# A list-scheduled attention and MLP kernel: the planner learns that VectorE and GpSimd exclude each other

## The chip, the cores and the metric

The kernel runs on one core of a Trainium2 chip. TensorE (PE in the profile) multiplies matrices and writes PSUM, VectorE (DVE) and ScalarE (ACT) read and write PSUM and SBUF, GpSimd (POOL) works on SBUF alone, and SyncE (SP) issues most of the DMAs. Each engine takes its instructions strictly in the order in which they stand in its queue. The metric is the device time of one execution in microseconds.

## The reference

Everything is fp32: 8 batches, 8 heads, 576 positions, head size 64, model size 512, hidden size 2048.

```python
kv  = einsum('bhsd,bhse->bhde', k, v)            # per head 64 x 64
o   = einsum('bhsd,bhde->bhse', q, kv)
x   = o / sqrt(mean(o*o, -1) + 1e-6) * g_norm    # heads side by side: 576 x 512
a1  = alpha1 * x + beta1
u   = x + lam * einsum('ts,bsd->btd', w_tok, a1) # token mixing, 576 x 576
a2  = alpha2 * u + beta2
out = u + lam * (relu(a2 @ w_ch1) @ w_ch2)
```

## The kernel before

**Stages of a batch.** k and v are loaded and rounded (`round_kv`, to `kr` and `vr`), and TensorE forms kv (`kv_groups`, L563). For batches 0 and 1 q is transposed on TensorE in fp32. From batch 2 on q is split into two bf16 halves: `split_q` writes the high half on ScalarE and the remainder, a subtraction, on VectorE or GpSimd (L510); `qt_dma` transposes both halves by DMA (L517). `qkv_groups` multiplies q by kv for two chunks of 128 positions at a time (a last one has 64), and then runs a chain: the square on ScalarE (L682), its sum on VectorE (L684), square root (L687), reciprocal (L690), the normalised x on VectorE (L706), `rt` = x times alpha1 lam g_norm as bf16 (L710), and at last x times g_norm in place on GpSimd (L712). `tok_groups` mixes the tokens: it needs all five chunks of `rt` and the transposed w_tok `wt` (L740); the result is added to x on VectorE (L722) and multiplied by alpha2 to `a2b` (L726), which `ut_groups` transposes to `a2t`. `ch1_groups` makes the hidden layer (L855 for even batches, L870 for odd ones, which also carry the tails of two batches; L886 for a first part of batch 0), with bias and relu on ScalarE or VectorE (L844, L845). `ch2_groups` multiplies by lam w_ch2 (L919), adds u (L928) and stores.

**How batches interleave.** While the hidden layer of batch b runs, the attention chain of batch b+1 is mixed in; then come the token mixing of b+1 and the second layer of b, into which the roundings, the q split and kv of batch b+2 are merged. So at each change of batch the chain up to `rt` of the next batch has to be finished when TensorE has come through the hidden layer.

**Head.** Batch 0 is handled in two halves of four heads. w_tok is loaded in natural order and cast to bf16 (`wt_groups`, part `cast`); the cast permutes columns so that every fourth column stands together, two more casts take the last 64 columns, and TensorE transposes 128 x 128 pieces (L1076, L1093). w_ch1 comes in four loads into three staging slots and is cast by whichever of three engines suits (L1173 and the cast behind it); w_ch2 likewise, multiplied by lam (L1186, L1191). Until the first hidden-layer matmul can start, the planner fills TensorE with dummy matmuls (L1265).

**What sets the order.** Nothing of this order is written out by hand. `Prog.op` records each operation with its engine or engines, an estimated cost for each, and its dependencies. `Prog.schedule` plays the operations through in model time: an engine that is free takes the ready operation of the lowest priority number (in SyncE's opening loads, strictly the first; TensorE looks at most eight ahead). Where several engines can do it, `better_elsewhere` asks whether another would be through sooner; GpSimd or VectorE operations carry a handicap of 0.7 us for VectorE (`spare`). `hasten` puts everything that the first hidden-layer matmuls depend on in the order of its remaining path, and `soon` keeps an engine free for such an operation. The plan's order becomes the queue of each engine; semaphores are added afterwards, so the order is fixed before the program runs and doesn't react to what happens on the chip. PSUM banks are handed out by the plan too.

Costs in microseconds for n elements per partition (the planner's own):

```python
def dve_us(n, mode=1): return 0.16 + n / 960.0 / mode
def act_us(n):         return 0.19 + n / 1200.0
def pool_us(n):        return 0.15 + n * 0.0024
def dve_pool(n):       return {"DVE": dve_us(n) + 0.08, "POOL": pool_us(n)}
```

In the plan VectorE and GpSimd work side by side without any effect on each other.

Of the kernel before, what the change touches and what calls it, by code (L numbers as in the profile page):

```python
# [9 lines left out]
ALU = mybir.AluOpType  # L10
# [12 lines left out]
class Op:  # L23
    __slots__ = ("eng", "cost", "fn", "deps", "alloc", "tiles", "pri", "idx",
                 "start", "end", "pos", "fixed", "waits", "inc", "lat", "ring", "clock")

    def __init__(self, eng, cost, fn, pri, idx):
        self.eng, self.cost, self.fn, self.pri, self.idx = eng, cost, fn, pri, idx
        self.deps, self.fixed = set(), False
# [20 lines left out]
class Prog:  # L50
# [20 lines left out]
    def op(self, eng, cost, fn, r=(), w=(), pri=0.0, dma_us=None, at=None, after=()):  # L71
# [3 lines left out]
        o.lat = dma_us  # L75
# [47 lines left out]
    def schedule(self):  # L123
# [10 lines left out]
        dma_free = 0.0  # L134
# [223 lines left out]
def bass_transnormer_attn__then__resmlp_affine_kernel(  # L358
# [15 lines left out]
    with ExitStack() as stack:  # L374
# [63 lines left out]
        def pool_us(n):  # L438
            return 0.15 + n * 0.0024
# [27 lines left out]
        def load_tail(n, b, at=None):  # L467
# [4 lines left out]
                w=[key], dma_us=1.2, at=at)  # L472
# [10 lines left out]
        def round_kv(b, parts=ALL, after=()):  # L483
            for i, hs in enumerate(parts):
                m = 256 * (hs.stop - hs.start)
                aa = halves(hs)
                for src, dst, lo, n in ((kf, kr, 0, "k"), (vf, vr, 64, "v")):
                    o, s = dst[:, 0:4, hs, :], src[:, hs].rearrange("p h c d -> p c h d")
                    ot, st = dst[0:64, 4, hs, :], kft[lo:lo + 64, hs]
                    P.op(act_dve(m, 1.7) if b < R32 else "DVE", dve_us(m, 1.7),  # L490
                         lambda e, o=o, s=s: copy(e, o, s),
                         r=[(n + "f", a) for a in aa], w=[(n + "r", a, 0) for a in aa],
                         after=after)
                    P.op(act_dve(m // 4, 1.7) if b < R32 else "DVE", dve_us(m // 4, 1.7),
                         lambda e, o=ot, s=st: copy(e, o, s),
                         r=[n + "ft"], w=[(n + "r", a, 1) for a in aa],
                         after=after)

        def split_q(b):

            lo_, par = 64 * (b % 2), b % 2
            for c in range(5):
# [8 lines left out]
                    out=lo, in0=src, in1=hi, op=ALU.subtract), r=kin + [kh], w=[kl])  # L511
# [43 lines left out]
        def kv_groups(b):  # L555
            def group(a):
# [35 lines left out]
                for h in range(2):  # L592
# [7 lines left out]
                        r=[("kvd", a, h, 0), ("kvd", a, h, 1)], w=[("kvd", a, h, 2)])  # L600
# [21 lines left out]
        def qkv_groups(b):  # L622

            def group(cs, hs):
# [74 lines left out]
                else:  # L699
# [9 lines left out]
                P.op(dve_pool(64 * m) if b else "DVE", dve_us(64 * m),  # L709
                     lambda e: e.tensor_tensor(out=r_, in0=x, in1=eb, op=ALU.mult),  # L710
                     r=xk + ["e1"], w=[("rt", rc(b, c), a) for a in aa for c in cs], pri=-100)
# [6 lines left out]
        def tok_out(b, c, t):  # L718
# [5 lines left out]
            if b == 0 and c < 4:  # L724
# [3 lines left out]
                r=xk + ["a2"], w=[("a2b", c) if c < 4 else ("a2bt", b % 2)])  # L728
# [237 lines left out]
        def params():  # L966
            P.op("DVE", 0.69, lambda e: e.tensor_tensor(
                out=e1r, in0=e1r, in1=lamr, op=ALU.mult), r=["lamr", "e1r"], w=["e1r"])
# [83 lines left out]
        def wt_groups():  # L1052
            def cast(tc):
                rr = 128 if tc < 4 else 64
                o = wsb[0:rr, tc, 0:512].rearrange("p (c s) -> p c s", c=4)
                i = wst[0:rr, tc, 0:512].rearrange("p (s c) -> p c s", c=4)
                P.op({"POOL": 0.75, "DVE": 0.75, "ACT": 0.65}, 0, lambda e: copy(e, o, i),
                     r=[("wst", tc)], w=[("wsb", tc)])

            def cast_tail(rr, tcs):  # L1060
                P.op({"POOL": 0.4, "DVE": 0.4, "ACT": 0.4}, 0, lambda e: copy(
                    e, wsb[0:rr, tcs, 512:576], wst[0:rr, tcs, 512:576]),
                    r=[("wst", tc) for tc in range(tcs.start, tcs.stop)],
                    w=[("wsbt", tcs.start)])
            for tc in range(5):
                yield lambda tc=tc: cast(tc)
            yield lambda: cast_tail(128, slice(0, 4))
            yield lambda: cast_tail(64, slice(4, 5))

            def group(tc):  # L1070
# [3 lines left out]
                def f(e):  # L1074
                    for sc in range(4):
                        m = e.transpose(  # L1076
                            t.flat().bitcast(BF16)[:, 128 * sc:128 * sc + rr],
                            wsb[0:rr, tc, 128 * sc:128 * sc + 128], identb[0:rr, 0:rr])
                    return m
# [7 lines left out]
            def group_tail():  # L1087
# [9 lines left out]
                P.op("PE", 0.35, f, r=["identb", ("wsbt", 0), ("wsbt", 4)], w=[t])  # L1097
# [65 lines left out]
        for key in ([("wst", x) for x in range(5)] + ["smask", ("wsbt", 0), ("wsbt", 4)] +  # L1163
# [7 lines left out]
        def load_w(i):  # L1171
            if i < 4:
# [4 lines left out]
                for dj in range(4):  # L1177
# [3 lines left out]
                        r=[("stg", i % 3)], w=[("w1p", i, dj)], at=-960.0 + i)  # L1181
                P.lastw[("w1", i)] = [y for dj in range(4) for y in P.lastw[("w1p", i, dj)]]
                bias_groups(i)
            else:
# [5 lines left out]
                for hh in range(4):  # L1190
# [3 lines left out]
                        after=u0)  # L1194
# [104 lines left out]
```

## Time and profile before

| what | us |
|---|---|
| median of three runs (397.54 to 399.26) | 398.19 |
| the profiled execution | 397.5 |
| span in that execution, first to last instruction | 395.4 |
| TensorE busy | 369.6 |
| VectorE busy | 252.5 |
| GpSimd busy | 148.5 |
| ScalarE busy | 147.6 |

A row such as "L510 DVE TENSOR_TENSOR qs<-qf,qs" names the line of the kernel, the engine, the operation and what it writes from what. In a timeline the first number is the start and the second the duration, both in microseconds; brackets show how long the engine had been idle just before and what ended that idle time. In the chain that ended last, pieces are given as start, duration and what ran. The time of an instruction on VectorE or GpSimd includes the time in which it has started but stands still. Casts and copies made through the helper `copy` carry L449 on ScalarE and L450 on the others, whatever they belong to; the tile names tell them apart (`kr`, `vr`, `wt`, `w`; w_tok's staging and bf16 copy lie in the memory of `ht` and are named so; the tails of k and v share the tile `kft`).

### The profile page before, as it was taken

To read this page: it belongs to the slowest core of one execution; us is meant where nothing else is said; L and a number is where in the kernel's file an instruction comes from. 1 tells how busy PE (TensorE), PEld (TensorE's weight loads), DVE (VectorE), ACT (ScalarE), POOL (GpSimd) and SP (SyncE) were. 2 spreads that over 40 slices of the span, in tenths; PEclk is the share of its full clock that TensorE was granted. 3 is DMA by queue.
4 is the path that set the end of the run, shared out by engine and by line. 5 is a ranking of instruction groups with operands and counts; after the bars stand their busy time and mean duration, and the time that the engine had idled before them with its cause. 6 is when DMAs were issued, how large, how long until landed. Compare 5 with 4: busy or idle time off the path is not lost.

```text
span 395.4 us, 5965 instructions
## 1 busy us (share of the span) xinstructions
PE 369.6 (93%) x2543; PEld 216.5 (55%) x2303; DVE 252.5 (64%) x367; ACT 147.6 (37%) x262; POOL 148.5 (38%) x108
## 2 busy tenths in 40 slices
PE   6999989879799899799988999899999999999995
PEld 4578766336564365346753465346774465447642
DVE  6569889998684648873799248873765248620021
ACT  1665646212753027501770017501760047006600
POOL 7357257970585303550175002650084005610000
PEclk9879999989999999999998999999999999999999
DMA  8987999768998539892975219832442110140012
GB/s 193 301 320 171 362 373 257 214 156 161 281 214 196 164 109 228 154 188 79 236 164 138 76 54 234 165 82 67 102 61 60 73 55 2 26 120 28 0 55 80
DMA packets 93948, 59.27 MB, mean 150 GB/s; under 512 B 60306, under 2 KB 84894, under 8 KB 93922
## 3 DMA queue, kind: packets, MB, share of 16 engines
q1 hardware_dynamic: 93888, 58.88, 60.3%
q8 instruction: 19, 0.31, 0.3%
q14 instruction: 7, 0.06, 0.0%
q10 hardware_dynamic: 34, 0.02, 0.0%
HBM read 38.04 MB, written 9.44 MB: 120 GB/s over the span
## 4 chain that ended last, share of the span: by engine, by line
PE 63%; DVE 14%; DMA 13%; ACT 3%; issue 2%; POOL 2%; SPq 1%; POOLq 0%
PE ps L919 26%; PE ps L870 11%; PE ps L740 9%; PE ps L855 7%; DMA stg<-in_moe_w_ch_dram 6%; DMA qf<-in_q_dram 6%; PE ps L563 4%; DVE qs L510 3%; DVE rt L710 2%; DVE small L684 2%; DMA qt<-qs 2%; DVE xm L706 2%; DVE w L1191 1%; PE ps L960 1%; PE ps L641 1%
## 5 line engine op out<-in xcount | busy, mean ns | idle before, releaser
L919 PE MATMUL ps<-w,ht 128*128 128x512 bf16 x576 | 131.4, 382 | 1.8 <-DVE xm L928 1.6
L919 PEld LDWEIGHTS ps<-w,ht 128*128 128x128 bf16 x576 | 55.3, 98 | 67.6 <-DVE xm L928 2.1
L844 ACT ACTIVATE ht<-ps,bias 128x640 bf16<-128x640 f32 (+2 forms) x98 | 71.0, 737 | 46.1 <-PE ps L870 36.5
L870 PE MATMUL ps<-a2t,w 128*128 128x320 bf16 x512 | 72.2, 299 | 2.6 <-ACT ht L844 1.6
L928 DVE TENSOR_TENSOR xm<-ps,xm 128x512 f32<-128x512 f32 x32 | 22.1, 690 | 70.4 <-PE ps L919 70.2
L870 PEld LDWEIGHTS ps<-a2t,w 128*128 128x128 bf16 x512 | 49.2, 98 | 23.0 <-ACT ht L844 2.6
L710 POOL TENSOR_TENSOR rt<-xm,e_bc 128x1024 bf16<-128x1024 f32 x7 | 16.5, 2355 | 116.6 <-DVE xm L706 116.6
L855 PE MATMUL ps<-a2t,w 128*128 128x512 bf16 x240 | 54.8, 379 | 1.7 <-ACT ht L844 1.7
L740 PE MATMUL ps<-rt,wt 128*128 128x512 bf16 x180 | 42.1, 391 | 8.9 <-DVE rt L710 5.3
L590 ACT ACTIVATE kvd<-ps 64x128 bf16<-64x128 f32 x24 | 6.5, 271 | 106.2 <-PE ps L563 106.1
L712 POOL TENSOR_TENSOR xm<-xm,g_bc 128x1024 f32<-128x1024 f32 (+1 forms) x18 | 40.8, 2266 | 12.6 <-DVE rt L710 11.8
L855 PEld LDWEIGHTS ps<-a2t,w 128*128 128x128 bf16 x240 | 22.5, 98 | 27.5 <-ACT ht L844 2.6
L740 PEld LDWEIGHTS ps<-rt,wt 128*128 128x128 bf16 x180 | 17.5, 100 | 32.1 <-DVE rt L710 6.6
L845 DVE TENSOR_SCALAR ht<-ps,bias 128x512 bf16<-128x512 f32 (+2 forms) x34 | 24.9, 747 | 8.9 <-PE ps L855 4.4
L684 DVE TENSOR_REDUCE small<-sq 128x16 f32<-128x1024 f32 (+3 forms) x27 | 25.0, 933 | 5.4 <-ACT sq L682 5.3
L563 PE MATMUL ps<-vr,kr 128*128 128x256 f32 x160 | 24.4, 301 | 3.4 <-DVE vr L450 3.4
L722 DVE TENSOR_TENSOR xm<-ps,xm 128x512 f32<-128x512 f32 x28 | 19.0, 686 | 11.7 <-PE ps L740 11.4
L726 POOL TENSOR_TENSOR a2b<-xm,a_bc 128x512 bf16<-128x512 f32 x15 | 19.4, 1291 | 17.1 <-DVE xm L722 16.9
L563 PEld LDWEIGHTS ps<-vr,kr 128*128 128x128 f32 x160 | 21.4, 193 | 6.0 <-DVE vr L450 4.2
L682 ACT ACTIVATE sq<-ps 128x1024 f32<-128x1024 f32 (+3 forms) x27 | 21.3, 797 | 8.4 <-PE ps L651 4.2
L510 DVE TENSOR_TENSOR qs<-qf,qs 128x512 bf16<-128x512 f32 x13 | 20.2, 1558 | 5.6 <-ACT qs L449 5.5
L449 ACT ACTIVATE qs<-qf 128x512 bf16<-128x512 f32 x24 | 14.2, 621 | 15.9 <-DMA qf<-in_q_dram 11.2
(112 smaller groups left out, 397.2 us busy)
## 6 DMA issues: line engine op xcount, KB each, us to landing
stg<-in_moe_w_ch_dram SPq DMA_DIRECT2D x8, 1024.0 KB, 12.7
out_dram<-xm SPq DMA_DIRECT2D x32, 256.0 KB, 2.4
kf<-in_k_dram SPq DMA_DIRECT2D x7, 1024.0 KB, 10.3
vf<-in_v_dram SPq DMA_DIRECT2D x7, 1024.0 KB
qf<-in_q_dram SPq DMA_DIRECT2D x7, 1024.0 KB, 6.5
ht<-in_moe_w_tok_dram SPq DMA_DIRECT2D x2, 576.0 KB, 9.0
kf<-in_k_dram SPq DMA_DIRECT2D x2, 512.0 KB, 7.2
kft<-in_k_dram SPq DMA_DIRECT2D x8, 128.0 KB, 4.7
```

What stands on the lines that cost most here:

```text
L510: P.op(dve_pool(512), 0, lambda e, hi=hi, lo=lo, src=src: e.tensor_tensor(out=lo, in0=src, in1=hi, op=ALU.subtract), r=kin + [kh], w=[kl])
L563: m = e.matmul(o, flat(kr[:, c, 2 * pr:2 * pr + 2, :]), flat(vr[:, c, 4 * a:4 * a + 4, :]), start=(c == 0), stop=(c == 4))
L684: P.op("DVE", dve_us(64 * m), lambda e: e.tensor_reduce(out=smv, in_=sqv, axis=AX.X, op=ALU.add), r=[("sq", sqs)], w=[("sm", sms)], pri=-20)
L710: lambda e: e.tensor_tensor(out=r_, in0=x, in1=eb, op=ALU.mult),
L712: P.op("POOL", pool_us(64 * m), lambda e: e.tensor_tensor(out=x3, in0=x3, in1=gb, op=ALU.mult), r=xk + ["g"], w=xk, pri=-50)
L740: m = e.matmul(t.flat(), wt[:, ws, tok_col(b, c):tok_col(b, c) + 128], rt[:, ws, :], start=(sc == 0), stop=(sc == 4))
L844: return e.activation(dst, src(), ACT.Relu, bias=bi)
L845: return e.tensor_scalar(out=dst, in0=src(), scalar1=bi, scalar2=0.0, op0=ALU.add, op1=ALU.max)
L855: m = e.matmul(t.flat(), w1[:, dj, 128 * fj:128 * fj + 128], a2t[:, dj, 0:512], start=(dj == 0), stop=(dj == 3))
L870: m = e.matmul(t.ap()[:, i, 0:320], w1[:, dj, 128 * fj:128 * fj + 128], a2t[:, dj, 320 * i:320 * i + 320], start=(dj == 0), stop=(dj == 3))
L919: m = e.matmul(t.flat(), ht[:, fj, 128 * c:128 * c + 128], w2[:, fj, :], start=(fj == 0), stop=(fj == 15))
L928: P.op("DVE", dve_us(512), lambda e: e.tensor_tensor(out=x, in0=t.flat(), in1=x, op=ALU.add), r=[t] + keys, w=keys)
```

## The change

- **Plan.** Operations that read or write SBUF on both of VectorE's port pairs, or take both inputs from SBUF, are marked `port=True`. In the plan such an operation on VectorE and any operation on GpSimd exclude each other: neither starts while the other has more than 0.1 us to go, and one that starts sooner is pushed behind. `better_elsewhere` takes the time at which the port is free into account.
- **Costs.** GpSimd is counted at 0.12 + 0.0021 n; the tails of k, v and q at 1.5 us of transfer in place of 1.2; roundings at mode 1.8 in place of 1.7.
- **Engines.** `round_kv` may go to ScalarE or VectorE in all batches, not only in the first two. `rt` of batch 0 may go to GpSimd too, as in the later ones.
- **w_tok.** Each of five chunks is cast in one go, 576 columns without permuting, and the two casts of the last columns go; the transposes read every fourth column.

```diff
@@ schedule
-        dma_free = 0.0
+        dma_free = port_free = 0.0
...
-                at = max(t, free[e2])
+                at = max(t, free[e2], port_free if shared(o, e2) else 0.0)
...
+        def shared(o, e):
+
+            return e == "POOL" or (e == "DVE" and o.port)
...
+                        if port_free > t + 0.1 and shared(o, e):
+                            continue
...
                     free[e] = t + pick.cost
+                    if shared(pick, e):
+                        port_free = max(port_free, t) + pick.cost
+                        free[e] = port_free
...
-                        pick.end = t + pick.cost + (0.35 if e == "PE" else 0.15)
+                        pick.end = free[e] + (0.35 if e == "PE" else 0.15)
@@ costs and roundings
-            return 0.15 + n * 0.0024
+            return 0.12 + n * 0.0021
...
-                w=[key], dma_us=1.2, at=at)
+                w=[key], dma_us=1.5, at=at)
...
-                    P.op(act_dve(m, 1.7) if b < R32 else "DVE", dve_us(m, 1.7),
+                    P.op(act_dve(m, 1.8), 0,
                          lambda e, o=o, s=s: copy(e, o, s),
                          r=[(n + "f", a) for a in aa], w=[(n + "r", a, 0) for a in aa],
-                         after=after)
+                         after=after, port=True)
...
@@ rt
-                P.op(dve_pool(64 * m) if b else "DVE", dve_us(64 * m),
+                P.op(dve_pool(64 * m), 0,
                      lambda e: e.tensor_tensor(out=r_, in0=x, in1=eb, op=ALU.mult),
-                     r=xk + ["e1"], w=[("rt", rc(b, c), a) for a in aa for c in cs], pri=-100)
+                     r=xk + ["e1"], w=[("rt", rc(b, c), a) for a in aa for c in cs], pri=-100,
+                     port=True)
@@ wt_groups
-                o = wsb[0:rr, tc, 0:512].rearrange("p (c s) -> p c s", c=4)
-                i = wst[0:rr, tc, 0:512].rearrange("p (s c) -> p c s", c=4)
-                P.op({"POOL": 0.75, "DVE": 0.75, "ACT": 0.65}, 0, lambda e: copy(e, o, i),
-                     r=[("wst", tc)], w=[("wsb", tc)])
...
+                P.op({"POOL": 0.75, "DVE": dve_us(576, 1.6), "ACT": act_us(576)}, 0,
+                     lambda e: copy(e, wsb[0:rr, tc, 0:576], wst[0:rr, tc, :]),
+                     r=[("wst", tc)], w=[("wsb", tc)], port=True)
...
-                            wsb[0:rr, tc, 128 * sc:128 * sc + 128], identb[0:rr, 0:rr])
+                            wsb[0:rr, tc, sc:512:4], identb[0:rr, 0:rr])
```

`port=True` also stands on the roundings' tails, the subtraction of `split_q` (L510), the copies of kv to the other partitions (L598), the product for `a2b` (L726), one parameter product (L967), the casts of w_ch1 and the products for w_ch2 (L1191).

More of the change, by code (lines that the diff above doesn't have):

```diff
@@ L24 @@
     __slots__ = ("eng", "cost", "fn", "deps", "alloc", "tiles", "pri", "idx",
-                 "start", "end", "pos", "fixed", "waits", "inc", "lat", "ring", "clock")
+                 "start", "end", "pos", "fixed", "port", "waits", "inc", "lat", "ring", "clock")
     def __init__(self, eng, cost, fn, pri, idx):
         self.eng, self.cost, self.fn, self.pri, self.idx = eng, cost, fn, pri, idx
-        self.deps, self.fixed = set(), False
+        self.deps, self.fixed, self.port = set(), False, False
         self.alloc, self.tiles = [], []
@@ L69, in ptile, with op @@
         return PTile(self, n)
-    def op(self, eng, cost, fn, r=(), w=(), pri=0.0, dma_us=None, at=None, after=()):
+    def op(self, eng, cost, fn, r=(), w=(), pri=0.0, dma_us=None, at=None, after=(), port=False):
         if isinstance(eng, dict):
@@ L74, in op @@
         o = Op(eng, cost, fn, len(self.ops) + pri + self.bias, len(self.ops))
-        o.lat = dma_us
+        o.lat, o.port = dma_us, port
         if at is not None:
@@ L510, in split_q @@
                 P.op(dve_pool(512), 0, lambda e, hi=hi, lo=lo, src=src: e.tensor_tensor(
-                    out=lo, in0=src, in1=hi, op=ALU.subtract), r=kin + [kh], w=[kl])
+                    out=lo, in0=src, in1=hi, op=ALU.subtract), r=kin + [kh], w=[kl], port=True)
         def qt_dma(b):
@@ L727, in tok_out @@
                 out=a2b[rows, c, :], in0=x, in1=a2_bc[rows, :], op=ALU.mult),
-                r=xk + ["a2"], w=[("a2b", c) if c < 4 else ("a2bt", b % 2)])
+                r=xk + ["a2"], w=[("a2b", c) if c < 4 else ("a2bt", b % 2)], port=True)
         def tok_col(b, c):
@@ L967, in params @@
             P.op("DVE", 0.69, lambda e: e.tensor_tensor(
-                out=e1r, in0=e1r, in1=lamr, op=ALU.mult), r=["lamr", "e1r"], w=["e1r"])
+                out=e1r, in0=e1r, in1=lamr, op=ALU.mult), r=["lamr", "e1r"], w=["e1r"], port=True)
             P.op("DVE", 0.69, lambda e: e.tensor_tensor(
@@ L1096, in f @@
                     return m
-                P.op("PE", 0.35, f, r=["identb", ("wsbt", 0), ("wsbt", 4)], w=[t])
+                P.op("PE", 0.35, f, r=["identb"] + [("wsb", tc) for tc in range(5)], w=[t])
                 for ws in (4, 5):
@@ L1162, in bass_transnormer_attn__then__resmlp_affine_kernel @@
         run([wt_groups()])
-        for key in ([("wst", x) for x in range(5)] + ["smask", ("wsbt", 0), ("wsbt", 4)] +
+        for key in ([("wst", x) for x in range(5)] + ["smask"] +
                     [("wsb", tc) for tc in range(5)]):
@@ L1193, in load_w @@
                         op=ALU.mult), r=[("stg", i % 3), "lam"], w=[("w2p", n, hh)], pri=60,
-                        after=u0)
+                        after=u0, port=True)
                 P.lastw[("w2", n)] = [y for hh in range(4) for y in P.lastw[("w2p", n, hh)]]
```

15 lines of the change are left out of this document (4 added, 11 removed).

## The prediction

> **What bounds the kernel now.** I read the page's first part, then who waited for whom on TensorE, then the timelines of VectorE and GpSimd around each stall.
>
> ```profile
> span 395.4 us, 5965 instructions
> ...
> PE 369.6 (93%) x2543; PEld 216.5 (55%) x2303; DVE 252.5 (64%) x367; ACT 147.6 (37%) x262; POOL 148.5 (38%) x108
> ```
>
> TensorE is busy 93% of the span, so at most 395.4 - 369.6 = 25.8 us, and what a lowered clock costs, can be won without changing matmuls. The change alters no matmul but the w_tok transposes; what it brings must come out of these waits:
>
> ```profile
> PE ps L740 <- DVE rt L710: 5.3, 3, 2.1
> PE ps L740 <- DVE xm L722: 3.4, 1, 3.4
> ...
> PE ps L855 <- ACT ht L844: 1.7, 2, 0.9
> PE ps L870 <- ACT ht L844: 1.6, 1, 1.6
> PE ps L919 <- DVE xm L928: 1.6, 1, 1.6
> PE ps L870 <- DVE xm L706: 0.9, 1, 0.9
> ```
>
> The columns are total, times and longest. The first two rows, 8.7 us in four stalls, are token mixing (L740) waiting for VectorE at a change of batch. First the rows of one line on both engines (minimum/median/maximum ns), then one such stall:
>
> ```profile
> L510 DVE TENSOR_TENSOR qs<-qf,qs x13: 679/1450/2853, 88.3 to 256.3; 128x512 bf16<-128x512 f32 x13
> L510 POOL TENSOR_TENSOR qs<-qf,qs x11: 1151/1157/1570, 81.7 to 250.3; 128x512 bf16<-128x512 f32 x11
> ```
>
> ```profile
> 203.97 2.68 POOL L712 TENSOR_TENSOR xm<-xm,g_bc 128x1024 f32<-128x1024 f32 x1 [1.23 <-DVE rt L710]
> ```
>
> ```profile
> 204.34 2.85 DVE L510 TENSOR_TENSOR qs<-qf,qs 128x512 bf16<-128x512 f32 x1
> 207.12 0.19 DVE L690 RECIPROCAL small<-small 64x8 f32<-64x8 f32 x1
> 207.35 0.68 DVE L706 TENSOR_TENSOR xtl<-ps,small 64x512 f32<-64x512 f32 x1
> 208.06 0.68 DVE L710 TENSOR_TENSOR rt<-xtl,e_bc 64x512 bf16<-64x512 f32 x1
> ```
>
> ```profile
> 208.81 2.74 PE L740 MATMUL ps<-rt,wt 128*128 128x512 bf16 x6 [2.06 <-DVE rt L710]
> ```
>
> One and the same VectorE subtraction (L510) takes 0.68 or up to 2.85 us. The long one ends at 207.19, 0.54 us after the GpSimd multiply that it overlaps (206.65): it stood still until GpSimd was through. The reciprocal and the x write queued behind it, though they use nothing that GpSimd held, and rt behind them. So the two engines exclude each other, as the new planner assumes; the old plan counted that subtraction at 0.77 us.
>
> **The change part by part.** *A: the stall at 77.88.* VectorE, GpSimd, TensorE, then the chain that ended last:
>
> ```profile
> 72.12 2.29 DVE L450 CAST kr<-kf 128x2048 fp32r<-128x2048 f32 x1
> 74.33 2.57 DVE L450 CAST kr<-kft 64x512 fp32r<-64x512 f32 x1
> 76.83 1.21 DVE L450 CAST vr<-vf 128x2048 fp32r<-128x2048 f32 x1
> 78.07 2.45 DVE L450 CAST vr<-kft 64x512 fp32r<-64x512 f32 x1
> ```
>
> ```profile
> 73.41 6.83 POOL L712 TENSOR_TENSOR xm<-xm,g_bc 128x1024 f32<-128x1024 f32 x2
> ```
>
> ```profile
> 81.30 1.47 PE L740 MATMUL ps<-rt,wt 128*128 128x512 bf16 x5 [3.42 <-DVE xm L722]
> ```
>
> ```profile
> 82.77 3.20 PE ps L919 x8
> ...
> 208.81 7.08 PE ps L740 x25
> ...
> 296.70 5.40 PE ps L740 x25
> ```
>
> ```profile
> L450 DVE CAST kr<-kft x9: 274/408/2570, 7.4 to 278.3; 64x512 fp32r<-64x512 f32 x6, 64x256 fp32r<-64x256 f32 x3
> ```
>
> Four roundings take 2.29 + 2.57 + 1.21 + 2.45 = 8.5 us; the third ran free in 1.21, and a tail's median is 0.41, so 3.2 would do. The surplus of 5.3 exceeds the stall of 3.42: the x additions (L722) that free the PSUM banks queued behind it. ScalarE may now take roundings, and a plan that knows the exclusion can put L722 first. After the stall 13 matmuls take 1.47 + 3.20 = 4.67 us; at 5.40/25 = 0.216 each they would take 2.81. A is worth 3.42 + 1.86 = 5.3 at most.
>
> *B, C, D: three batch changes.* B and D by VectorE's timeline, then windows (length, PE busy, granted clock, DMA share, GB/s):
>
> ```profile
> 163.19 2.78 DVE L510 TENSOR_TENSOR qs<-qf,qs 128x512 bf16<-128x512 f32 x1
> ...
> 252.82 2.77 DVE L510 TENSOR_TENSOR qs<-qf,qs 128x512 bf16<-128x512 f32 x1
> ```
>
> ```profile
> 160.00:169.00 9.00, 6.54 (x30) 1.00 0.83 140
> 204.00:216.00 12.00, 9.78 (x44) 0.86 0.31 96
> ```
>
> The three waits for rt are 5.3 us; C (at 206.75) is 2.06 of it, so B (at 166.65) and D (at 256.07) are 3.2 together. In each of B and D 2.78 - 0.68 = 2.1 us is standing still, more than the stall; without that subtraction in that place both vanish: 3.2. At C the reciprocal could start at about 204.8 and the x write end at 205.7, but rt needs the port, which GpSimd holds to 206.65: rt ends at 207.3 instead of 208.74, so order alone wins 1.4 of 2.06. The 25 matmuls after C took 7.08 against 5.40 later, at a clock of 0.86; at B it stayed at 1.00. So another 1.7 goes if the rest of the stall, 0.6, leaves the clock up as B did. C is worth 3.1.
>
> The Trainium skill, "TensorE: Matmul & The Clock Gate", Part 1, lowers the clock only after an idle window of about 3.4 us. By that rule C would have cost no clock and its removal would bring 1.4; the trace shows that 2.06 us was enough, so the sum keeps 3.1.
>
> *E.* The last wait row is L706 behind another subtraction that GpSimd delayed:
>
> ```profile
> 106.63 1.26 DVE L510 TENSOR_TENSOR qs<-qf,qs 128x512 bf16<-128x512 f32 x1 [2.10 <-ACT qs L449]
> ```
>
> At most 1.26 - 0.68 = 0.6 comes back. Sum of order alone: 5.3 + 3.2 + 3.1 + 0.6 = 12.2. The rows of ACT ht and xm L928, 4.9 us, I leave standing: the exclusion isn't in them.
>
> *What is late next.*
>
> ```profile
> 77.88:131.43 53.55, 46.93 (x346) 28.16 (x306) 41.55 (x54) 21.07 (x36) 30.95 (x20) 0.97 0.90 197
> ```
>
> From 78 to 131 us the DMA engines are busy 0.90 of the time (second last column), so a start earlier by A runs into loads for the next batches that don't come earlier by as much. I give A half, 2.7 (bounds 0 and 5.3). Around C the share is 0.31, and B to D stand. That leaves 9.5.
>
> *Roundings on ScalarE in all batches.*
>
> ```profile
> L449 ACT ACTIVATE qs<-qf 128x512 bf16<-128x512 f32 x24 | 14.2, 621 | 15.9 <-DMA qf<-in_q_dram 11.2 <-DMA qt<-qs 4.6
> ...
> L449 ACT ACTIVATE kr<-kf 128x1024 fp32r<-128x1024 f32 x1 | 1.1, 1057 | 0.9 <-DMA kf<-in_k_dram 0.9
> ```
>
> From 512 to 1024 elements ScalarE adds 0.44 us, so 2048 is an estimated 1.93 against 1.21 on VectorE. Behind one, relu (L844) waits up to 1.93 us, and TensorE behind relu for PSUM. ScalarE is 37% busy and the planner moves a rounding only where it expects it to end sooner; I take nothing. Upper bound: one exposed rounding in each of six batches, 11.6 us; lower: the roundings' part in A, already counted.
>
> *The w_tok cast and the first batch.*
>
> ```profile
> L449 ACT ACTIVATE ht<-ht 128x512 bf16<-128x512 f32 x2 | 2.2, 1123 | 0.2 <-DMA ht<-in_moe_w_tok_dram 0.2
> ```
>
> ```profile
> 21.25 2.15 ACT L449 ACTIVATE wt<-ps 128x512 bf16<-128x512 bf16 x4 [2.01 <-PE ps L1076]
> ```
>
> ```profile
> 32.61 2.35 PE L759 MATMUL ps<-rt,wt 128*128 128x256 bf16 x20
> ```
>
> ```profile
> L651 PEld LDWEIGHTS ps<-kvr,qtr 128*128 128x128 f32 x48 | 5.7, 192 | 0.2
> ...
> L1076 PEld LDWEIGHTS ps<-identb,ht 128*128 128x128 bf16 x16 | 1.2, 119 | 1.5 <-issue 1.5
> ```
>
> The main copies of wt end at 23.4 and token mixing starts at 32.61: nine microseconds hide the cheaper cast, so 0; without them it could save at most the 1.12 that a permuted cast took, since the five run on three engines. The strided weight read of 20 transposes is unseen: between 119 ns and the slowest load, 192, so 0 to +1.5 us; no gain, since as many columns load. I take 0, for the same nine microseconds cover it.
>
> By the Trainium skill, "TensorE: Matmul & The Clock Gate", § Weight-path perf modes, the fast weight load also takes strided columns, which would make the upper end 0; no run here shows it yet.
>
> On the path to the first hidden layer an rt of batch 0 loses time to the exclusion:
>
> ```profile
> 32.75 1.74 DVE L710 TENSOR_TENSOR rt<-xm,e_bc 128x512 bf16<-128x512 f32 x1
> ```
>
> 1.74 - 0.68 = 1.06 may come back. But GpSimd may now take the rt of batch 0; at L510's medians, 1.16 against 0.68, four of them are 1.9 lost. I take 0, bounds -1.1 and +1.9.
>
> So 9.5. A new order over all queues will misjudge elsewhere, above all loads of q, k and v, still priced as before; I charge one new stall as long as C, 2.1. Net -7.4. The profiled execution took 397.5 (the span and 2.1 around it), 0.7 below the median of 398.19; against that median 390.8.
>
> **The rivals.** *R1, slower: GpSimd first.* The planner's loop over engines reaches POOL before DVE (POOL's first operation stands first in the program). Whenever the port comes free GpSimd may take a low-priority subtraction ahead of VectorE's urgent rt, again and again. For: rt and subtractions are ready together at each batch change. Against: the subtractions become ready one by one behind ScalarE's halves, and TensorE's plan can run second-layer matmuls meanwhile. Price: two subtractions of 1.16 late at each of seven changes, beyond what those matmuls cover: 16.2 less the 9.5, +6.7, 404.9. It decides from about eight uncovered subtractions on (9.5/1.16).
>
> *R2, nothing.* The same port work lies in the same stretch, stalls move between the queues of DVE and POOL, loads set the rest: 398.2. For: GpSimd holds the port 2.35 us at a time whatever the order. Against: B and D vanish by order alone.
>
> *R3, half.* A is given back wholly to the loads and C keeps its slow clock: 1.4 + 3.2 + 0.6 less 2.1 is -3.1, 395.1. For: the DMA share of 0.90. Against: loads start earlier too.
>
> **How the numbers follow.** Forecast 0.43, R3 0.24, R2 0.16, R1 0.17. Faster by over 0.5%, 2 us, about what a measurement here tells from no change: forecast and R3, 0.67; within it: R2, 0.16; slower: R1, 0.17. The forecast's own range is 386.0 (all 12.2) to 394. With the head's 1.1 as well it is 384.9 at the low end; the high end, 401, takes in R2 and R1 with half its price.
>
> **What would show it.** Right: no subtraction of over 1.5 us on VectorE ahead of rt; the waits of L740 for rt and xm L722 down from 8.7 to under 3 us; roundings at 72 us no longer one blocked row; clock 1.00 after the third batch change; the first hidden layer still near 42 us. Wrong: rt later than the second layer can cover (R1), as much waiting under other names (R2), or stalls between 95 and 131 us grown by what A gave (R3).

## The result

The changed kernel takes 384.0 us against 398.0 of the kernel before: ratio 0.964, 95% interval 0.958 to 0.969, 14 us. The forecast was 390.8, its range 384.9 to 401.0: the direction was right, the gain nearly twice as large, and the time just outside the range. Times and ratios from here on leave out disturbed runs, those over 1.5% above their kernel's fastest, with a lower granted clock; e10's profile is of such a run. The profiled execution took 383.6 with a span of 381.8, 13.6 below the span of before.

The page's first part, changed kernel:

```profile
span 381.8 us, 5989 instructions
...
PE 369.2 (97%) x2534; PEld 220.4 (58%) x2326; DVE 198.0 (52%) x323; ACT 160.9 (42%) x266; POOL 193.6 (51%) x146
```

TensorE works as long as before in a shorter span. VectorE is busy for 54 us less, GpSimd for 45 us more, ScalarE for 13 more: standing still counted as busy, and work has moved. Who waited for whom on TensorE (total, times, longest; in this kernel's line numbers L750 is token mixing, L865 and L880 the hidden layer, L929 the second layer, L854 relu on ScalarE):

```profile
PE ps L1267 <- POOL ident L1038: 2.0, 1, 2.0
PE ps L865 <- ACT ht L854: 1.7, 1, 1.7
PE ps L572 <- ACT vr L458: 0.9, 1, 0.9
PE ps L572 <- DVE vr L459: 0.5, 1, 0.5
```

No row of L750 is left: the 8.7 us for which token mixing waited are gone altogether. So are the rows of xm L928 and L706, and of relu 1.7 us remains in place of 3.3.

The subtraction that stood still is the same line on the two engines as before, L519 now (minimum/median/maximum in ns):

```profile
L519 POOL TENSOR_TENSOR qs<-qf,qs x16: 1153/1158/1496, 90.6 to 253.4; 128x512 bf16<-128x512 f32 x16
L519 DVE TENSOR_TENSOR qs<-qf,qs x8: 693/1032/1928, 91.4 to 247.1; 128x512 bf16<-128x512 f32 x8
```

VectorE does 8 in place of 13, with a median of 1.03 us in place of 1.45 and nothing above 1.93. At the batch change that was C, GpSimd, VectorE and TensorE now read:

```profile
197.13 2.36 POOL L719 TENSOR_TENSOR rt<-xm,e_bc 128x1024 bf16<-128x1024 f32 x1
199.56 1.59 POOL L719 TENSOR_TENSOR rt<-xtl,e_bc 64x512 bf16<-64x512 f32 x1
201.24 2.35 POOL L722 TENSOR_TENSOR xm<-xm,g_bc 128x1024 f32<-128x1024 f32 x1
```

```profile
198.31 0.67 DVE L715 TENSOR_TENSOR xtl<-ps,small 64x512 f32<-64x512 f32 x1
198.90 1.13 DVE L519 TENSOR_TENSOR qs<-qf,qs 128x512 bf16<-128x512 f32 x1
203.35 0.69 DVE L732 TENSOR_TENSOR xm<-ps,xm 128x512 f32<-128x512 f32 x1 [3.31 <-PE ps L750]
```

```profile
199.69 2.54 PE ps L929 x11
202.23 5.40 PE ps L750 x25
```

```profile
200.00:212.00 12.00, 11.95 (x57) 5.40 (x57) 5.82 (x9) 0.47 (x1) 11.42 (x8) 1.00 0.20 41
```

Both rt stand on GpSimd, back to back, and are through at 201.15. TensorE, whose order comes from the same plan, does second-layer matmuls of the old batch until then and starts token mixing at 202.23 without a gap; 25 matmuls take 5.40 us at a clock of 1.00 (before: 7.08 at 0.86). VectorE idles for 3.31 us. GpSimd has taken the critical products, slower, and nobody waits: the plan had put enough second-layer matmuls ahead of token mixing.

*Where the time came from.* The start of each batch's hidden layer in the two timelines, and the difference:

| batch | before, us | after, us | difference | change since the row above |
|---|---|---|---|---|
| 0 | 42.42 | 45.93 | +3.5 | +3.5 |
| 1 | 95.37 | 94.44 | -0.9 | -4.4 (A lies here, see below) |
| 2 | 145.78 | 139.70 | -6.1 | -5.2 (E, and the rows ACT ht and xm L928) |
| 3 | 186.52 | 179.92 | -6.6 | -0.5 (B, less a relu stall of 1.7) |
| 4 | 235.56 | 224.71 | -10.9 | -4.3 (C) |
| 5 | 276.12 | 262.46 | -13.7 | -2.8 (D) |
| 7 | 356.26 | 342.61 | -13.7 | 0 |

Two things beside A lie between batches 0 and 1. In the kernel before, TensorE also waited there for a rounding of v; the prediction leaves that row out. The row has 1.78 us in the head and 1.64 at 51.17; in the changed kernel 0.86 is left of the second.

```profile
PE ps L563 <- DVE vr L450: 3.4, 2, 1.8
```

And the clock, which was 0.50 after A in the kernel before (82.2 to 85.6 us), is so in the changed kernel too, from 66.0 to 69.5 us, though no stall of over 0.3 us stands in the 12 us ahead of it (windows as in the prediction; the third column from the end is the granted clock):

```profile
62.60:66.00 3.40, 3.40 (x31) 3.19 (x31) 1.28 (x2) 2.05 (x2) 3.24 (x3) 1.00 1.13 307
66.10:69.40 3.30, 3.08 (x8) 1.11 (x8) 1.92 (x3) 1.78 (x4) 3.07 (x4) 0.50 1.11 253
```

Half of these 3.4 us, 1.7, is an estimate of what it costs. So A's 3.42 of stall and 1.86 of clock and 0.8 of the other row were won, less 1.7: 4.4.

### The profile page after: what moved, and what is told of

Read it like the earlier page. It is cut to its first block, busy times and chain, and to the rows that moved or that the text cites. A ratio compares the mean times of both kernels' runs of the same rounds, so it can differ in the third digit from the quotient of the medians.

```text
span 381.8 us, 5989 instructions
## 1 busy us (share of the span) xinstructions
PE 369.2 (97%) x2534; PEld 220.4 (58%) x2326; DVE 198.0 (52%) x323; ACT 160.9 (42%) x266; POOL 193.6 (51%) x146
## 4 chain that ended last, share of the span: by engine, by line
PE 74%; DMA 10%; POOL 5%; DVE 3%; SPq 3%; ACT 3%; issue 1%; POOLq 0%
PE ps L929 26%; PE ps L880 15%; PE ps L865 10%; PE ps L750 9%; DMA qf<-in_q_dram 9%; PE ps L572 3%; PE ps L650 2%; PE ps L360 2%; PE ps L970 1%; PE ps L660 1%; POOL a2b L736 1%; POOL rt L719 1%; POOL xm L722 1%; DMA qt<-qs 1%; SPq L526 1%
## 5 line engine op out<-in xcount | busy, mean ns | idle before, releaser
L929 PE MATMUL ps<-w,ht 128*128 128x512 bf16 x557 | 126.2, 379 | 1.1
L929 PEld LDWEIGHTS ps<-w,ht 128*128 128x128 bf16 x576 | 55.2, 98 | 64.3
L854 ACT ACTIVATE ht<-ps,bias 128x640 bf16<-128x640 f32 (+2 forms) x90 | 65.3, 732 | 44.9 <-PE ps L880 32.8
L719 POOL TENSOR_TENSOR rt<-xm,e_bc 128x1024 bf16<-128x1024 f32 (+1 forms) x15 | 31.0, 2066 | 93.5 <-DVE xm L715 93.0
L880 PE MATMUL ps<-a2t,w 128*128 128x320 bf16 x512 | 71.8, 299 | 0.1
L880 PEld LDWEIGHTS ps<-a2t,w 128*128 128x128 bf16 x512 | 49.4, 98 | 19.8 <-ACT ht L854 0.5
L865 PE MATMUL ps<-a2t,w 128*128 128x512 bf16 x230 | 54.8, 387 | 2.4 <-ACT ht L854 1.7
L855 DVE TENSOR_SCALAR ht<-ps,bias 128x512 bf16<-128x512 f32 (+2 forms) x42 | 32.2, 773 | 18.3 <-PE ps L865 8.8
L722 POOL TENSOR_TENSOR xm<-xm,g_bc 128x1024 f32<-128x1024 f32 (+1 forms) x18 | 38.4, 2131 | 3.9 <-DVE rt L719 2.7
L750 PE MATMUL ps<-rt,wt 128*128 128x512 bf16 x178 | 39.7, 379 | 0.1
L865 PEld LDWEIGHTS ps<-a2t,w 128*128 128x128 bf16 x240 | 23.1, 100 | 28.5 <-issue 2.2
L736 POOL TENSOR_TENSOR a2b<-xm,a_bc 128x512 bf16<-128x512 f32 x27 | 35.6, 1318 | 5.1 <-DVE xm L732 3.1
L750 PEld LDWEIGHTS ps<-rt,wt 128*128 128x128 bf16 x180 | 17.5, 98 | 21.1 <-POOL rt L719 0.3
L519 POOL TENSOR_TENSOR qs<-qf,qs 128x512 bf16<-128x512 f32 x16 | 18.9, 1179 | 9.4 <-ACT qs L458 8.2
## 6 DMA issues: line engine op xcount, KB each, us to landing
stg<-in_moe_w_ch_dram SPq DMA_DIRECT2D x8, 1024.0 KB, 12.3
```

What stands on the lines that cost most here:

```text
L722: P.op("POOL", pool_us(64 * m), lambda e: e.tensor_tensor(out=x3, in0=x3, in1=gb, op=ALU.mult), r=xk + ["g"], w=xk, pri=-50)
L736: P.op(dve_pool(512), 0, lambda e: e.tensor_tensor(out=a2b[rows, c, :], in0=x, in1=a2_bc[rows, :], op=ALU.mult), r=xk + ["a2"], w=[("a2b", ...
L750: m = e.matmul(t.flat(), wt[:, ws, tok_col(b, c):tok_col(b, c) + 128], rt[:, ws, :], start=(sc == 0), stop=(sc == 4))
L854: return e.activation(dst, src(), ACT.Relu, bias=bi)
L855: return e.tensor_scalar(out=dst, in0=src(), scalar1=bi, scalar2=0.0, op0=ALU.add, op1=ALU.max)
L865: m = e.matmul(t.flat(), w1[:, dj, 128 * fj:128 * fj + 128], a2t[:, dj, 0:512], start=(dj == 0), stop=(dj == 3))
```

## The experiments

All ratios are against the kernel before, run beside on the same chip. "Waits" are those of token mixing on TensorE in the profiled execution, "start" the first hidden-layer matmul.

Runs of one kernel differ by some 4 us, and the granted clock differs with them: of the changed kernel's four, the fastest took 381.43 at a mean clock of 0.990 and the slowest 385.53 at 0.975. The column "x clock" is the mean of time multiplied by granted clock over a kernel's runs, an estimate of the time at full clock; 377.6 and 375.9 for these two. The kernel before, beside the runs e1 to e18, gives 388.2 to 389.6.

| run | what | us | x clock | ratio, interval | waits | start |
|---|---|---|---|---|---|---|
| after | the change | 384.0 | 376.1 | 0.964, 0.958 to 0.969 | 0 | 45.9 |
| e1 | before, exclusion alone | 388.5 | 379.7 | 0.979, 0.972 to 0.987 | 0 | 42.8 |
| e2 | after without exclusion | 387.3 | 380.9 | 0.974, 0.968 to 0.980 | 2.0 | 44.3 |
| e3 | after, VectorE chooses first | 383.3 | 380.0 | 0.966, 0.959 to 0.973 | 5.1 | 43.2 |
| e4 | after, rt of batch 0 on VectorE | 381.4 | 376.3 | 0.959, 0.953 to 0.965 | 0 | 50.2 |
| e5 | before, old order, short g product | 384.6 | 379.2 | 0.969, 0.962 to 0.976 | 0 | 42.4 |
| e6 | before, roundings alone | 386.9 | 380.2 | 0.977, 0.969 to 0.984 | 3.0 | 41.5 |
| e7 | before, GpSimd's cost alone | 385.9 | 381.6 | 0.974, 0.968 to 0.981 | 3.3 | 40.0 |
| e8 | after, roundings on VectorE | 390.5 | 383.2 | 0.985, 0.977 to 0.993 | 0.2 | 44.6 |
| e9 | before, tail cost alone | 395.8 | 388.1 | 0.997, 0.992 to 1.001 | 6.1 | 45.6 |
| e10 | before, w_tok cast alone | 393.4 | 386.3 | 0.990, 0.985 to 0.995 | 6.9 | 48.8 |
| e11 | before, ScalarE cost 0.20 | 387.9 | 381.0 | 0.977, 0.971 to 0.983 | 3.4 | 43.9 |
| e12 | after, ScalarE cost 0.20 | 381.6 | 375.6 | 0.962, 0.956 to 0.969 | 0 | 43.3 |
| e13 | e2, ScalarE cost 0.20 | 386.2 | 379.6 | 0.974, 0.965 to 0.984 | 1.6 | 44.1 |
| e14 | e2, ScalarE cost 0.18 | 386.1 | 381.1 | 0.974, 0.967 to 0.981 | 2.1 | 42.3 |
| e15 | after, ScalarE cost 0.18 | 385.7 | 376.8 | 0.973, 0.965 to 0.982 | 0.2 | 41.9 |
| e16 | before, ScalarE cost 0.18 | 395.0 | 384.1 | 0.994, 0.989 to 0.998 | 6.8 | 44.1 |
| e17 | e4, ScalarE cost 0.20 | 379.6 | 373.0 | 0.955, 0.948 to 0.962 | 0 | 44.1 |
| e18 | after, own order, short g product | 382.6 | 376.1 | 0.962, 0.953 to 0.971 | 0 | 44.2 |

**Does standing still behind GpSimd cause the stalls?** e5 keeps every queue in its old order and takes the length from the GpSimd product that VectorE stood behind; it leaves g_norm out of most columns.

```diff
-                    out=x3, in0=x3, in1=gb, op=ALU.mult)
+                    out=x3[..., 0:1], in0=x3[..., 0:1], in1=gb[..., 0:1], op=ALU.mult)
```

> The kernel before with every queue in exactly its old order, but GpSimd's product of x and g_norm (L712) executed on the first of each head's 64 columns only, so that it holds the port for a small part of its 2.35 us; x of the other columns is left without g_norm. If the stalls A to D (8.7 us of waits plus about 3.5 of lowered clock) come from VectorE standing still behind GpSimd (the prediction's cause): 383 to 389 us and waits of token mixing for rt and xm L722 under 2 us. Rival: VectorE has too much work of its own in these stretches, the standing still only fills time: 394 to 399 us, waits of 5 us or more.

```profile
L510 DVE TENSOR_TENSOR qs<-qf,qs x13: 673/693/1944, 83.8 to 242.9; 128x512 bf16<-128x512 f32 x13
```

```profile
PE ps L870 <- ACT ht L844: 1.7, 1, 1.7
...
PE ps L855 <- ACT ht L844: 1.5, 2, 0.8
PE ps L919 <- DVE xm L928: 1.4, 1, 1.4
PE ps L870 <- DVE xm L706: 0.9, 1, 0.9
```

The 13 subtractions on VectorE, in the same places as before, now have a median of 0.69 us in place of 1.45; no wait of token mixing is left, and the time falls by 12.3 us (396.8 beside it). The prediction's sum of order alone is 12.2; the ratio's interval leaves 9.6 to 15.1. The rows that it didn't count are still there with 4.6 us, and so is the 0.9 of E. The product itself takes 0.22 us (median) in place of 2.35. By the starts of the hidden layers (42.43, 90.76, 140.98, 179.79, 224.79 and 263.48 for batches 0 to 5), the change from batch to batch is -4.6 (A), -0.2 (E), -1.9 (B), -4.0 (C) and -1.9 (D). So with the old order fixed, the time for which GpSimd holds the port in this product costs about what the prediction said. The subtractions and rt don't use its result, so they stood behind the hold and not behind missing data. The theory stands and its rival, that VectorE simply has too much to do, falls for the waits of token mixing.

e18 makes the same cut in the changed kernel's own order.

> The changed kernel in its own order, with GpSimd's product of x and g_norm executed on the first of each head's 64 columns only (x of the other columns is left without g_norm), as in e5. The old order won 12 us by that. If the changed order no longer stands behind GpSimd: 382 to 385 us, at most 2 won. If much of the waiting only moved: 375 to 380 us.

It won 1.4 us by the medians (0.962 against 0.964, the intervals overlap) and nothing at equal clock (376.1 in both): the changed order hardly stands behind that product any more.

**Which part of the change does it?**

```diff
 e1: before, plus shared(), port_free and port=True; old costs, old engines, old cast
 e2: after, with
-            return e == "POOL" or (e == "DVE" and o.port)
+            return False
```

> The kernel before with the exclusion of VectorE's two-port operations and GpSimd in the plan, and nothing else of the change (old costs, old engine choices, old w_tok cast). Theory X (the gain is the plan's knowledge of the exclusion): 382 to 388 us, token mixing no longer waits for rt and xm L722 (under 2 us in place of 8.7). Rival Y (the gain is the moved work: roundings on ScalarE, cheaper GpSimd in the plan): 393 to 399 us, at least half of the 8.7 us of waits left.

> The changed kernel with the plan's exclusion switched off; costs, engine choices and the w_tok cast stay changed. Theory X: 394 to 400 us, as before, with VectorE instructions standing still again (subtractions of 1.5 to 2.9 us). Rival Y: 384 to 389 us.

Neither X nor Y: each half wins 8 to 11 of the 14 us by itself. In e1 no wait of token mixing is left, as X has it, but other stalls came in:

```profile
PE ps L865 <- DMA a2t<-a2b: 4.3, 1, 4.3
PE ps L880 <- DVE kvd L604: 3.0, 1, 3.0
```

In e2 VectorE stands still as X has it, yet TensorE waits little for it:

```profile
L519 DVE TENSOR_TENSOR qs<-qf,qs x7: 1150/1637/2650, 85.7 to 244.3; 128x512 bf16<-128x512 f32 x7
```

```profile
PE ps L835 <- DVE a2t L459: 2.7, 1, 2.7
PE ps L572 <- DVE vr L459: 2.6, 2, 1.6
PE ps L750 <- POOL rt L719: 2.0, 2, 1.8
```

So I took the remaining edits one at a time.

```diff
 e6: before, with
-                    P.op(act_dve(m, 1.7) if b < R32 else "DVE", dve_us(m, 1.7),
+                    P.op(act_dve(m, 1.7), 0,
 e7: before, with
-            return 0.15 + n * 0.0024
+            return 0.12 + n * 0.0021
 e9: before, with
-                w=[key], dma_us=1.2, at=at)
+                w=[key], dma_us=1.5, at=at)
 e10: before, with the cast of 576 columns and wsb[0:rr, tc, sc:512:4] in the transposes
```

> The kernel before with one thing of the change: roundings of k and v may go to ScalarE in every batch. The prediction priced this at nothing. Theory Z (seen from the run without the exclusion: stall A went because ScalarE took roundings near 72 us): A's 5.3 us go, B to D stay, 391 to 395 us. Rival (it moves nothing by itself): 396 to 400 us.

> The kernel before with one thing of the change: GpSimd counted at 0.12 + 0.0021 n. GpSimd then takes more of the products and VectorE fewer. Theory (the lower price, not the exclusion, is what empties VectorE): 388 to 394 us and VectorE's busy time down by 15 us or more. Rival (without the exclusion a cheaper GpSimd only meets VectorE more often): 396 to 402 us.

> The kernel before with one thing of the change: transfers of the tails of k, v and q counted at 1.5 us in place of 1.2 in the plan. It has nothing to do with the exclusion. Theory U (the order before was an unlucky one, with subtractions and roundings put just behind GpSimd's long products; almost any new plan leaves that): 384 to 390 us. Rival V (what won in the earlier runs was the particular edit): 395 to 400 us.

> The kernel before with the unpermuted w_tok cast and the strided transposes alone. The prediction priced the cast at nothing and the strided weight read at 0 to 1.5 us. By theory U the plan is drawn anew here too: 384 to 391 us. By rival V: 396 to 400 us. In either case the weight loads of the w_tok transposes tell the price of the stride: 119 ns on average if it is free, towards 192 if not.

e6 won 10 us, twice what Z allowed it: the roundings near 70 us do go to ScalarE,

```profile
68.15 1.91 ACT L449 ACTIVATE kr<-kf 128x2048 fp32r<-128x2048 f32 x1
69.95 0.61 ACT L449 ACTIVATE kr<-kft 64x512 fp32r<-64x512 f32 x1
70.47 1.90 ACT L449 ACTIVATE vr<-vf 128x2048 fp32r<-128x2048 f32 x1
```

but the later stalls shrank too, since the whole order was drawn anew. e7 won 11 us, with VectorE only 9.5 us less busy (252.5 to 243.0), so its reason as written, VectorE emptied by 15 us or more, isn't borne out. Its time, 385.9, is below the ranges of both expectations. The tail cost moved nothing that can be told, the cast about 1%: 393.4 lies between the ranges of U and V. What won is thus not one edit; and not every new order wins, which limits theory U.

**Is it the edit or the new draw?** The fixed cost of ScalarE in the plan, 0.19 us, means nothing to the exclusion. Set to 0.18 and 0.20 it draws the order anew in three kernels.

```diff
-            return 0.19 + n / 1200.0
+            return 0.20 + n / 1200.0
```

> The kernel before with ScalarE's fixed cost in the plan 0.20 in place of 0.19 us, a change that means nothing to the exclusion and is no part of the change. Theory U: 384 to 392 us. Rival V: 395 to 400 us.

> The kernel before with ScalarE's fixed cost 0.18: the third plan of the old kernel, after 398 and 387.9 (cost 0.20). Theory U, that 398 was unlucky: 386 to 393 us. If the old planner's usual result is near 396 and 387.9 was lucky: 394 to 400 us.

> The changed kernel without the exclusion in its plan, ScalarE's fixed cost 0.20. With e2 (387.3) and the next run a set of plans without the exclusion, against 384.0, 381.6 and e15 with it. If the exclusion is worth something beyond a new draw of the order: 386 to 392 us, at least 3 above the runs with it, with VectorE standing still before token mixing. If not: 380 to 386 us.

> As the run before, fixed cost 0.18. The same two expectations: 386 to 392 us if the exclusion counts by itself, 380 to 386 if any new draw of the order does.

> The changed kernel with ScalarE's fixed cost in the plan 0.20 in place of 0.19 us. If the changed plan avoids the stalls by what it knows: 382 to 387 us, with little of token mixing waiting for VectorE. If its 384 is one draw among plans spread over ten microseconds: anywhere from 381 to 392 us.

> The changed kernel with the exclusion, ScalarE's fixed cost 0.18. If the exclusion counts by itself: 380 to 386 us as the two plans before it. If plans with it spread as widely as those without: anywhere to 392.

| plan | 0.18 | 0.19 | 0.20 |
|---|---|---|---|
| kernel before | 395.0 | 398.0 | 387.9 |
| change without exclusion | 386.1 | 387.3 | 386.2 |
| change with exclusion | 385.7 | 384.0 | 381.6 |
| kernel before, x clock | 384.1 | 388.2 to 389.6 | 381.0 |
| without exclusion, x clock | 381.1 | 380.9 | 379.6 |
| with exclusion, x clock | 376.8 | 376.1 | 375.6 |

A meaningless hundredth of a microsecond is worth 10 us in the old planner, so part of the 14 us is that 398.0 was its worst order of the three; but 395.0 and e9's 395.8 are close to it, so 398 isn't far off its usual result either. The plans without the exclusion lie within 1.2 us of each other, about 7 us below the mean of the old ones (393.6). With the exclusion the mean is 383.8, 2.7 us lower: 4.6 and 3.3 us in two pairs, 0.4 in the third, with overlapping intervals. At equal clock the three pairs agree, 4.3, 4.8 and 4.0: the twelve runs with the exclusion lie between 374.7 and 378.4, the eleven without between 379.2 and 382.8. So the exclusion by itself adds about 4 us on top of the other edits, by this estimate; whether a plan also changes the clock, four runs of each don't tell. The wait that it was written for agrees in every pair: token mixing waits 0.2, 0 and 0 us with it, 2.1, 2.0 and 1.6 without, 6.8, 8.7 and 3.4 in the old planner.

**GpSimd first (the prediction's R1).** e3 lets the planner's loop reach VectorE first.

```diff
-            for e, q in queues.items():
+            for e, q in sorted(queues.items(), key=lambda kv: kv[0] != "DVE"):
```

> The changed kernel, but the planner's loop reaches VectorE before all other engines, so at a free port VectorE chooses first. If GpSimd's first choice costs anything (the prediction's R1, now as a loss inside a gain): 380 to 383 us. If the order of choice doesn't matter because TensorE's plan covers it: 384 within 2. If letting VectorE choose makes rt and VectorE's queue longer: above 386.

```profile
PE ps L750 <- DVE xm L938: 5.1, 2, 2.6
```

```profile
L519 DVE TENSOR_TENSOR qs<-qf,qs x13: 691/1539/2835, 86.8 to 240.6; 128x512 bf16<-128x512 f32 x13
```

383.3 us is by the medians the second expectation, no difference. But its runs had the higher granted clock (0.982 to 0.991 against 0.975 to 0.990): at equal clock it takes 380.0 against 376.1, 3.9 us more. VectorE is given 13 subtractions again and stands still up to 2.8 us, and token mixing waits 5.1. That GpSimd chooses first, which I had feared, is a gain here, probably because it keeps short work off the queue that everything urgent stands in.

**The first batch.** e4 binds the rt of batch 0 to VectorE.

```diff
-                P.op(dve_pool(64 * m), 0,
+                P.op(dve_pool(64 * m) if b else "DVE", dve_us(64 * m),
```

> The changed kernel with the rt of batch 0 bound to VectorE, as before. The changed kernel starts its first hidden layer at 45.9 us in place of 42.4. If rt on GpSimd makes that delay (the prediction's bound of +1.9 us, and more by what queues behind): start at 42 to 44 us and 380.5 to 382.5 us. If the delay comes from elsewhere in the first 45 us: start within 0.7 us of 45.9 and 384 within 1.5.

My reason fell: the start came 4 us later still, at 50.2, and yet the kernel is not slower (381.4; at equal clock 376.3 against 376.1). Over all runs the start lies between 40.0 and 50.2 us and shows no bearing on the total: e7 with 40.0 takes 385.9, e4 with 50.2 takes 381.4. What delays the start in the changed kernel stays open. The granted clock goes with it: from 0 to the start it is 0.92 in the kernel before, 0.89 in the changed one and 0.86 in e4; no run separates this from the order.

**Roundings on ScalarE in the changed kernel.** e8 takes them back, from batch 2 on, as the inverse of e6's diff.

> The changed kernel with the roundings from batch 2 on bound to VectorE again. If the exclusion in the plan is enough by itself for the batch changes: 383 to 386 us as the changed kernel. If ScalarE's roundings carry stall A: 387 to 390 us, with a stall near 78 us of 2 us or more.

390.5 is just above the second expectation's range, and its reason isn't there: no stall stands near 78 us. Its one large stall is relu behind a late load:

```profile
PE ps L880 <- ACT ht L854: 5.8, 1, 5.8
```

```profile
101.13 11.24 DMA qf<-in_q_dram
...
112.39 0.63 ACT qs L458
...
113.70 0.69 ACT ht L854
```

The load of q takes 11.2 us, ScalarE's next q half waits for it, and relu and TensorE behind that. The plan prices that load at 3 us. So e8 doesn't show that ScalarE's roundings carry A; it shows that in another order TensorE waits 5.8 us behind a late load.

**A faster version.** e17 puts e4 and e12 together.

> Looking for a version faster than both: the changed kernel with the rt of batch 0 on VectorE (e4, 381.4) and ScalarE's fixed cost 0.20 (e12, 381.6). If the two gains are real and add: 378 to 380 us. If they are draws of the order: 381 to 387 us.

379.6 us is the fastest of all, 4.5% below the kernel before; its interval overlaps with that of the changed kernel. With waits of TensorE of only 3.4 us in all (2.0 of them at the very start) it is near what this TensorE work allows. At equal clock it takes 373.0 us against 376.1, with runs from 372.5 to 373.6 against 375.1 to 377.6, so the kernel is faster; but e4 (376.3) and e12 (375.6) by themselves are not clear of 376.1. Its gain was met by drawing orders, and I don't call its two edits improvements.

## Why the prediction was wrong

- **The cause was right.** VectorE stood still behind GpSimd, and what queued behind it came late: e5 took the hold away in the old order and won 12.3 us where the sum said 12.2. That the two agree so closely is luck: A gave 4.6 against 5.3, B and D together 3.8 against 3.2, C 4.0 against 3.1 and E 0.2 against 0.6, each within a microsecond. C was undersized because the sum left 0.6 of its stall standing.
- **First failed step: "A half", -2.7.** I argued that the loads, at a DMA share of 0.90, would take half of A back. They took nothing. In e5, where the order is the old one, A's 4.6 us are won up to batch 1 and 0.2 more up to batch 2, where the giving back should have shown; in the changed kernel 5.2 us more are won there. R3 falls with it.
- **Second failed step: "the rows of ACT ht and xm L928, 4.9 us, I leave standing: the exclusion isn't in them".** For L928 the trace of before, which I hadn't read at that place, speaks against it (VectorE's and GpSimd's timelines, kernel before):

```profile
127.66 1.45 DVE L510 TENSOR_TENSOR qs<-qf,qs 128x512 bf16<-128x512 f32 x1
129.03 0.67 DVE L722 TENSOR_TENSOR xtl<-ps,xtl 64x512 f32<-64x512 f32 x1
129.63 1.15 DVE L510 TENSOR_TENSOR qs<-qf,qs 128x512 bf16<-128x512 f32 x1
130.70 1.64 DVE L726 TENSOR_TENSOR a2b<-xtl,a_bc 64x512 bf16<-64x512 f32 x1
132.27 0.68 DVE L928 TENSOR_TENSOR xm<-ps,xm 128x512 f32<-128x512 f32 x1
```

```profile
127.29 2.94 POOL L726 TENSOR_TENSOR a2b<-xm,a_bc 128x512 bf16<-128x512 f32 x2 [3.21 <-DVE xm L722]
130.31 1.49 POOL L510 TENSOR_TENSOR qs<-qf,qs 128x512 bf16<-128x512 f32 x1
```

  The three long ones stand still behind GpSimd too, 1.45 + 1.15 + 1.64 - 3 x 0.68 = 2.2 us, ahead of the L928 that TensorE waited 1.6 for. No run takes this hold away by itself: it comes from other products than e5's, and in e5 1.4 of the wait stands. In the changed kernel the row is gone. Of the waits for relu 1.7 us remain of 3.3; why, no run shows.
- **Third: the charges for the new order.** I took 0 for the first batch and 2.1 for a new stall. The first hidden layer came 3.5 us later, beyond my bound of 1.9; after it the only stall of over 1 us is relu's 1.7 at 154.7, where 0.9 stood before. That new stalls can come is shown by e1, with 4.3 and 3.0 us.
- **The arithmetic.** -12.2, +2.7 and +2.1 gave -7.4; the span fell by 13.6, which is 6.2 more. By the two traces that is the 2.7 that A didn't give back, 3.2 of the rows left standing (4.9 less the 1.7 that remain), 0.8 of the row of L563 that the prediction passed over, 1.0 for the whole of the stalls C and E in place of a part, 0.4 of the charge of 2.1 (the halved clock at 66 us took 1.7), and 1.6 that I can't assign; less the 3.5 by which the first hidden layer came later. The terms mis-sized are "A half" and the rows put at nothing; only the first has a run of its own, e5. The low bound (386.0 less 1.1 for the head) held every term of the order but not these rows, hence a range that ended 0.9 us too high.
- **The clock.** Without the stall at C the clock stayed at 1.00 there. That "2.06 us was enough" holds for this one stall and is no threshold: the clock was halved after stalls of 1.97 us (e18) and 2.03 us (e11), but not after 2.62 and 2.45 us in e3 (TensorE's timeline, then the window around it):

```profile
160.81 5.56 PE L750 MATMUL ps<-rt,wt 128*128 128x512 bf16 x24 [2.62 <-DVE xm L938]
```

```profile
158.00:168.00 10.00, 7.33 (x34) 3.32 (x35) 6.76 (x9) 0.00 (x0) 6.23 (x5) 1.00 0.67 172
```

  In the changed kernel it was halved at 66 us without such a stall. So an idle window of 3.4 us, as in the Trainium skill, "TensorE: Matmul & The Clock Gate", Part 1, is not needed in these traces, and the length of a stall alone doesn't say whether the clock falls.
- **The small prices held.** A permuted cast took 1.12 us, an unpermuted one of 576 columns 0.68; a rounding of 2048 on ScalarE was estimated at 1.93 and takes 1.90. The strided weight loads, 0 to 73 ns each by my bounds, took 138 ns on average in place of 119. But such an average mixes two clocks. Here are eight loads each (minimum/median/maximum ns): packed in the kernel before and strided in e15 at a clock of 1.00, then packed before and strided in the changed kernel at 0.50:

```profile
L1076 PEld LDWEIGHTS ps<-identb,ht x8: 97/98/102, 16.5 to 16.9; 128*128 128x128 bf16 x8
L1078 PEld LDWEIGHTS ps<-identb,ht x8: 111/114/133, 16.6 to 17.0; 128*128 128x128 bf16 x8
...
L1076 PEld LDWEIGHTS ps<-identb,ht x8: 102/151/151, 20.6 to 21.2; 128*128 128x128 bf16 x8
L1078 PEld LDWEIGHTS ps<-identb,ht x8: 113/147/147, 19.2 to 19.8; 128*128 128x128 bf16 x8
```

  The stride costs 16 ns a load at full clock and nothing at half. By the Trainium skill's section on weight-path perf modes in that same page the fast load also takes strided columns; here the price for 20 loads is at most 20 x 16 ns = 0.3 us. That it is hidden was not tested.

- **What was not asked.** I took one measured kernel for the old planner's result. e11 shows that a hundredth of a microsecond in an unrelated cost moves it by 10 us (by 8 at equal clock). A forecast for a planner needs that spread in its range.

## What to carry to other kernels

Read long instructions of one engine against their own minimum: where the same shape takes 0.68 and 2.85 us, the difference is waiting, and the damage is done by what queues behind it, not by the engine's load. When a planner writes the queues, judge an edit to it over several neutral redraws (a hundredth on an unrelated cost), since one pair of orders can differ by 10 us for no reason, and compare times at equal granted clock, with which much of the spread between runs of one kernel went here (e4: 4.6 us between its runs, 1.4 after multiplying by the clock). And when stalls go, read what stands ahead of the neighbouring stalls before you put them at nothing or charge for what might come back.

## What was not expected of the hardware

GpSimd's products take about twice as long as VectorE's (rt of 1024 columns 2.36 us on GpSimd; 1.23 on VectorE at 70.97 in the kernel before), and it now does 24 of the 27 rt in place of 11; the kernel became faster all the same, with VectorE busy for 198 us in place of 252 and GpSimd for 194 in place of 148. Where TensorE's order holds other work until the product is done, as at 199.69 to 202.23, the slower engine cost nothing.
